# An attention, expert and SwiGLU kernel: four edits to the order of its first 110 microseconds

## The chip, the core and the metric

The kernel runs on one core of one Trainium2 chip. The metric is the device time of one execution in microseconds, the median of the runs made. One more execution was recorded by the hardware profiler; all rows in this document are from it.

## What is computed

Three layers follow each other. First a linear attention with a decaying state, for 2 batches, 8 heads, 768 tokens and a head dimension of 48:

```python
for t in range(S):
    cur = np.einsum('bhd,bhe->bhde', u[None] * kt, vt)
    y[:, :, t] = np.einsum('bhd,bhde->bhe', rt, state + cur)
    state = wt[:, :, :, None] * state + np.einsum('bhd,bhe->bhde', kt, vt)
```

Its output is taken as 1536 tokens of 384 numbers. Each goes to the one of 8 experts with the largest gate logit, in the order of the tokens, as long as the expert has places; an expert is `relu(x @ w1) @ w2` with 1024 hidden numbers, scaled by the token's softmax weight. The last layer is `(silu(x @ w_gate) * (x @ w_val)) @ w_out` with 1536 hidden numbers. Inputs and output are fp32.

## The kernel before, in words

**Stages.** The tokens are cut into 12 units of 128 (u = 0 to 11). The first stage, up to about 108 us, runs the attention, the gate and the placing of tokens; the eight experts follow, then the last layer. The order of the instructions of each engine is the order in which the code issues them; `tc.manual_schedule()` leaves it alone. Tiles come from rotating buffers, and each instruction waits on semaphores for what it reads and overwrites.

**One unit of attention.** VectorE turns the decays into running products: `prep1` (line 363 `X`, a scan; 368 `anch`) and `prep2` (406 `R`, a scan; 412 and 415 `M`; 425 `rk`). TensorE multiplies keys with queries in `scores` (460, `psA`), ScalarE copies them out (462) and GpSimd blanks the upper triangle (463, `A`). `kgtok` turns the keys (471). `values` (485 and 490, `y`) is the attention's output, `state` (502 `psP`; VectorE 505 `d`, 510 `Sa`, 513 `Sc`) carries the state to the next unit, `expand` copies it (521, `Sb`). Each token's own term comes from `diag` and `columns`: a product with `fold` (570) into the small tile `lg`, copied by ScalarE (572, `a`), multiplied with the values by `own` (440, `aV`, on GpSimd). `xrow` (527) adds both into the unit's row `x`. `gate_t` turns it (541), `logits` (565) multiplies by the gate.

**The loop.** The loop over u = 0 to 9 does, in this order: `xrow(u-1)`, `state(u)`, idle products on TensorE (`warm`, line 449: 128 by 512 columns, read by nobody), `scores(u+1)`, `kgtok(u+1)`, `prep1(u+2)`, `gate_t(u-1)`, `prep2(u+2)`, `values(u)`, `columns` and `own` for u+1. Groups of units (0 to 3, 4 to 7, 8 and 9, 10 and 11) are chosen and counted together (`choose`, `count`, `place`), and `scatter` writes their weighted rows `xg` to their experts' places in DRAM (`scr`), by an indirect DMA on GpSimd's queue.

**The tail** (u = 10, written out by hand) finishes units 10 and 11. Expert 0's rows do not go through DRAM for units 8 to 11: `onehot` (790, `hot`) builds a matrix from a unit's places, and `x0_add` (810) sums row times matrix into three PSUM tiles `x0`. The rows of units 0 to 7 are loaded back from `scr` (`x0_load`, 784, into `zrow`) and added by a product with the identity. For units 10 and 11 a row is split into two fp32r halves, `x0_high` (799, ScalarE) and `x0_low` (804, VectorE). Units 8 and 9 use the fp32 row `xg`. `parts` (815, 816) splits the sum into `xe`, which expert 0 multiplies (1270, `psh`).

**Weights.** SyncE's queue loads raw weights (169, 768 KB each) into rotating buffers. ScalarE makes the high half (207), VectorE the low half (212) into `wu`; `fill(us)` places as many such steps as a budget allows. Buffers freed by `early.close()` allow three more raw loads.

Of the kernel before, what the change touches and what calls it, by code (L numbers as in the profile page):

```python
# [33 lines left out]
RAWS = 5, 2, 3  # L34
# [8 lines left out]
def build(tc, cap, dm, tk, vt, ub, cst, wg, w1, w2, wgate, wval, wout, out):  # L43
# [738 lines left out]
    def x0_load():  # L782
        for a, (s0, n) in enumerate(PARTS):
            nc.sync.dma_start(out=zrow[0:n, DM * a:DM * a + DM], in_=scr[s0:s0 + n, :])
# [82 lines left out]
    for u in range(NU - 2):  # L867
# [3 lines left out]
        if u:  # L871
            prep0(u + 2)
        warm((7, 4)[u] if u < 2 else 3, ps1, "xT")
        scores(u + 1)
# [25 lines left out]
        if u:  # L900
            values(u)
            columns(u - 1, max(u - 2, 0), u + 1)
            own(u + 1)
        else:
            values(u, [0, 1])
            for q in range(2):
                columns(q, q, q)
                own(q)
            values(u, [2, 3])
        if chosen:  # L910
# [30 lines left out]
    prep3(u + 1)  # L941
    early.close()
    more_raws(RAWS[2])
    load_raws(len(raws_))
    values(u, [2])
# [16 lines left out]
    columns(u - 1, u - 2, u + 1)  # L962
    xrow(u)
    rows4[2]()
    own(u + 1, nc.vector)
    gate_t(u)
    values(u + 1, [1, 2])
    c2, sums2, rows2, _ = chosen_of(two)
    for f in c2:
        f()  # L970
    rows4[3]()
    for q in (*ready, *four):
        scatter(q)
    x0_load()
    for f in sums2:
        f()
    count(two)
    at2, bases, placed, later = place(two)
    for f in (*bases, *placed):
        f()  # L980
    fill(1.2, 3.0)
    values(u + 1, [3])
    for f in rows2:
        f()
    xrow(u + 1)
    logits(u)
    for i in range(2):
        onehot(i, *(x[:, i, :] for x in at2))
    gate_t(u + 1)
    x0_add(xgs[two[0]], R(hot[0][:, 0, :]), 0, first=True, ks=[0])  # L990
    judge()
    tc.mark_branch_hint_location("rare", engines=[PE, SP])
    logits(u + 1)
    for f in later:
        f()
    for q in two:
        scatter(q)
    flush()
    fill(0.6, 3.0)
    x0_add(xgs[two[0]], R(hot[0][:, 0, :]), 0, first=True, ks=[1, 2])  # L1000
    c, sums, rows, sm = chosen_of(last)
# [4 lines left out]
    for f in (*bases, *sums):  # L1006
        f()
    tc.mark_branch_hint_location("rare", engines=[DVE, ACT, POOL])
    for i, q in enumerate(last):
# [5 lines left out]
    totals(ps1, ones, (ohacc, *(ohs[:, q, :] for q in (*two, *last))), odds)  # L1015
    x0_add(xgs[two[1]], R(hot[0][:, 1, :]), 0)
    for i, q in enumerate(last):
# [3 lines left out]
    x0_add(xhl[last[0]][1], hot[0][:, 2, :], 0)  # L1021
    offsets(one8)
    for f in rows:
        f()
# [499 lines left out]
```

## Time and profile before

| | |
|---|---|
| median of 3 runs | 473.61 us (472.63 to 474.22) |
| the profiled execution | 477.16 us, its span 475.4 us |
| TensorE matmul busy | 454.4 us (96%) |
| VectorE busy | 335.0 us (70%) |
| ScalarE busy | 239.8 us (50%) |
| mean granted TensorE clock | 0.976 of full speed |

A busy time of matmuls says that TensorE had some in flight, not that it ran at its peak, so stages are read one by one: which engine is busy all the time in a stretch, and what ends the waits of the others. In the page's slices of the span the granted clock is below full speed in three places, at about 19 to 26, 70 to 74 and 94 to 105 us. The two levels of TensorE's clock are 1.2 and 2.4 GHz. In the rows, PE is TensorE's matmul, DVE VectorE, ACT ScalarE, POOL GpSimd and SPq SyncE's DMA queue; L490 is line 490 of the kernel before.

### The profile page before, as it was taken

What the parts mean: (1) busy time and instruction counts of PE and PEld (TensorE: products, weight loads), DVE (VectorE), ACT (ScalarE), POOL (GpSimd) and SP (SyncE); (2) the same over time, 40 slices, a digit from 0 to 9 for tenths busy, and PEclk for the clock granted to TensorE, in tenths of its full rate; (3) what the DMA queues carried; (4) which work ended last, traced back from release to release, by engine and by line L of the source; (5) the groups of instructions that cost most, each with busy time, mean ns of one, the idle gap of its engine ahead of it and who ended that gap; (6) DMA issues with size and microseconds to landing.
All of it is one profiled execution on the core that took longest, in us unless ns stands there. A gap on an engine that the chain in (4) does not pass through costs nothing.

```text
span 475.4 us, 9312 instructions
## 1 busy us (share of the span) xinstructions
PE 454.4 (96%) x3572; PEld 401.8 (85%) x3572; DVE 335.0 (70%) x723; ACT 239.8 (50%) x560; POOL 72.6 (15%) x87
## 2 busy tenths in 40 slices
PE   7899889888999999999999999999999999999994
PEld 3587668678999999999988888888888888888884
DVE  8889999677798658559779966575868576434241
ACT  4466676636788677665455465353625333221220
POOL 3334445621000000000000370000000000003033
PEclk9899998959999999999999999999999999999999
DMA  7877996564989965027323425042200000001011
GB/s 241 234 236 205 361 270 186 184 215 135 293 272 345 305 239 175 24 67 219 115 77 123 71 64 122 11 123 77 66 2 1 1 0 0 1 0 68 0 68 66
DMA packets 33649, 62.57 MB, mean 132 GB/s; under 512 B 5216, under 2 KB 16992, under 8 KB 33600
## 3 DMA queue, kind: packets, MB, share of 16 engines
q1 hardware_dynamic: 31680, 57.20, 39.2%
q0 software_dynamic: 1920, 4.73, 2.7%
q8 instruction: 29, 0.48, 0.4%
q14 instruction: 20, 0.16, 0.1%
HBM read 52.48 MB, written 9.44 MB: 130 GB/s over the span
## 4 chain that ended last, share of the span: by engine, by line
PE 79%; DVE 10%; issue 4%; ACT 2%; DMA 2%; POOL 1%; another core or an unknown queue 0%; POOLq 0%; SPq 0%; DVEq 0%; ACTq 0%
PE psg L1381 31%; PE psu L1404 14%; PE psh L1270 14%; PE pso L1288 14%; DVE R L406 2%; DVE X L363 1%; PE psA L460 1%; DMA scr<-zrow 1%; POOL out L1416 1%; DVE M L415 1%; DVE M L412 1%; PE psx L1255 1%; PE y L490 1%; PE psW L449 1%; DVE rk L425 1%
## 5 line engine op out<-in xcount | busy, mean ns | idle before, releaser
L1381 PE MATMUL psg<-yb,wu 128*128 128x512 f32 x648 | 156.3, 395 | 0.0
L1381 PEld LDWEIGHTS psg<-yb,wu 128*128 128x128 f32 x648 | 121.5, 188 | 26.0
L1404 PE MATMUL psu<-wu,a 128*128 128x384 f32 x432 | 80.8, 336 | 0.0
L1404 PEld LDWEIGHTS psu<-wu,a 128*128 128x128 f32 x432 | 76.4, 188 | 2.9
L1270 PE MATMUL psh<-xe,wu 128*128 128x240 f32 x576 | 69.1, 277 | 1.4 <-DVE xe L816 1.4
L1270 PEld LDWEIGHTS psh<-xe,wu 128*128 128x128 f32 x576 | 66.2, 190 | 1.7 <-issue 1.6
L1288 PE MATMUL pso<-h,wu 128*128 128x240 f32 x576 | 66.4, 275 | 0.0
L1288 PEld LDWEIGHTS pso<-h,wu 128*128 128x128 f32 x576 | 65.3, 190 | 0.0
L1388 DVE TENSOR_TENSOR t<-t,psg 128x512 f32<-128x512 f32 x36 | 24.7, 686 | 52.6 <-PE psg L1381 35.6
L212 DVE TENSOR_TENSOR wu<-raw,wu 128x512 fp32r<-128x512 f32 x96 | 61.7, 683 | 0.0
L207 ACT CAST wu<-raw 128x512 fp32r<-128x512 f32 x96 | 55.0, 620 | 3.1 <-PE pso L1288 1.4
L1393 ACT CAST a<-t 128x512 fp32r<-128x512 f32 x36 | 22.3, 618 | 58.2 <-DVE t L1388 55.9
L1277 DVE SCALAR_TENSOR_TENSOR h<-psh,h 128x240 fp32r<-128x240 f32 x64 | 25.0, 403 | 24.1 <-ACT h L1276 23.8
L1303 POOL DMA_INDIRECT idl<-ids,dests x12 | 13.5, 1122 | 163.6 <-DVE bits L187 160.3
L1416 POOL DMA_INDIRECT out<-acc,idc x12 | 11.7, 973 | 174.1 <-DVE acc L1414 172.3
L207 ACT CAST wu<-bits 128x384 fp32r<-128x384 f32 x36 | 18.0, 514 | 40.0 <-DVE bits L200 39.2
L1387 ACT ACTIVATE t<-psg 128x512 f32<-128x512 f32 x36 | 21.4, 596 | 27.5 <-PE psg L1381 27.5
L1394 DVE TENSOR_TENSOR a<-t,a 128x512 fp32r<-128x512 f32 x36 | 24.8, 689 | 11.7 <-ACT a L1393 11.0
L1276 ACT ACTIVATE h<-psh 128x240 fp32r<-128x240 f32 x64 | 23.2, 372 | 11.0 <-PE psh L1270 10.2
L1414 DVE TENSOR_TENSOR acc<-psu,acc 128x384 f32<-128x384 f32 x24 | 12.9, 558 | 20.8 <-PE psu L1404 20.8
L462 ACT COPY A<-psA 128x512 f32<-128x512 f32 x24 | 12.9, 588 | 25.3 <-PE psA L460 23.0
L463 POOL TENSOR_SCALAR_AFFINE_SELECT A<-A 128x512 f32<-128x512 f32 x24 | 19.5, 834 | 27.5 <-ACT A L462 27.5
(153 smaller groups left out, 566.9 us busy)
## 6 DMA issues: line engine op xcount, KB each, us to landing
raw<-in_moe_w SPq DMA_DIRECT2D x32, 768.0 KB, 9.0
dm<-in_dm SPq DMA_DIRECT2D x18, 291.0 KB, 6.1
scr<-zrow SPq DMA_DIRECT2D x12, 384.0 KB, 5.4
raw<-in_moe_w_gate SPq DMA_DIRECT2D x6, 768.0 KB, 5.9
raw<-in_moe_w_val SPq DMA_DIRECT2D x6, 768.0 KB, 4.3
raw<-in_moe_w_out SPq DMA_DIRECT2D x6, 768.0 KB, 4.3
v<-in_tk SPq DMA_DIRECT2D x12, 192.0 KB, 6.7
dm<-in_dm SPq DMA_DIRECT2D x3, 512.0 KB, 5.7
```

Source lines behind the costliest of these rows:

```text
L207: nc.scalar.copy(out=slot_t[u % NSLOT][:, 0, c:c + n], in_=bits[i])
L212: nc.vector.tensor_tensor(out=w[:, 1, c:c + n], in0=bits.pop(i), in1=R(w[:, 0, c:c + n]), op=ALU.subtract)
L1270: nc.tensor.matmul(ps, w[:, a, k, c0:c0 + 128], xet[e][:, b, k, :], start=n == 0, stop=n == 8)
L1276: nc.scalar.activation(out=h[:, 0, :], in_=ps, func=AF.Relu)
L1277: nc.vector.scalar_tensor_tensor(out=h[:, 1, :], in0=ps, scalar=0.0, in1=R(h[:, 0, :]), op0=ALU.max, op1=ALU.subtract)
L1288: nc.tensor.matmul(ypt[e, d], w[:, a, f % 4, 128 * d:128 * d + 128], h[:, b, :], start=f == 0 and n == 0, stop=f == 7 and n == 2)
L1381: nc.tensor.matmul(gps[i][g], w[:, a, g, k, c0:c0 + 128], yb[t, k][:, c], start=a_ == k == 0, stop=a_ == k == 2)
L1387: nc.scalar.activation(out=t, in_=pg[0], func=AF.Silu)
L1388: nc.vector.tensor_tensor(out=t, in0=t, in1=pg[1], op=ALU.mult)
L1393: nc.scalar.copy(out=a[:, 0], in_=t)
L1394: nc.vector.tensor_tensor(out=a[:, 1], in0=t, in1=R(a[:, 0]), op=ALU.subtract)
L1404: nc.tensor.matmul(out_ps[t, j], att[i][:, c, 128 * j:128 * j + 128], w[:, a, f % 4, :], start=f % FP == 0 and n == 0, stop=f % FP == FP - ...
```

## The change

Four edits, in the words of the code.

1. In the loop's first turn `values(0)` is issued whole, ahead of both products with `fold`, in place of half ahead and half behind. The two products write 8 columns each instead of 16, with no copy between them; one copy takes both results.
2. From u = 2 on, `warm` issues five idle products instead of three; two more stand in the tail.
3. `early.close()` and the three raw loads stand behind `x0_load` instead of ahead of it.
4. Units 8 and 9 enter `x0` as fp32r halves, as 10 and 11 do, and their `xg` rows, places (`later`) and scatters come later. Two steps of `fill` move: one ahead, in front of `own(u+1)`, one behind `offsets`.

```diff
--- before.py
+++ after.py
@@ -870,7 +870,7 @@
         state(u)
         if u:
             prep0(u + 2)
-        warm((7, 4)[u] if u < 2 else 3, ps1, "xT")
+        warm((7, 4)[u] if u < 2 else 5, ps1, "xT")
         scores(u + 1)
         expand(u)
         kgtok(u + 1)
@@ -902,11 +902,15 @@
             columns(u - 1, max(u - 2, 0), u + 1)
             own(u + 1)
         else:
-            values(u, [0, 1])
+            values(u)
             for q in range(2):
-                columns(q, q, q)
+                to = logits_to(q)
+                nc.tensor.matmul(to[:, 0:E], gss.pop(q), fold[:, E:2 * E], start=True, stop=True)
+            a8 = gp.tile([128, 2, H], F32, tag="a82", name="a82")
+            nc.scalar.copy(out=a8, in_=lgt[group[0]][:, 0:2, 0:E])
+            for q in range(2):
+                a8s[q] = a8[:, q, :]
                 own(q)
-            values(u, [2, 3])
         if chosen:
             flush()
             if u < NU - 3:
@@ -939,9 +943,6 @@
     count(four)
     xrow(u - 1)
     prep3(u + 1)
-    early.close()
-    more_raws(RAWS[2])
-    load_raws(len(raws_))
     values(u, [2])
     gate_t(u - 1)
     place(four)
@@ -961,43 +962,47 @@
     logits(u - 1)
     columns(u - 1, u - 2, u + 1)
     xrow(u)
+    fill(1.2, 3.0)
     rows4[2]()
     own(u + 1, nc.vector)
     gate_t(u)
     values(u + 1, [1, 2])
-    c2, sums2, rows2, _ = chosen_of(two)
+    c2, sums2, rows2, sm2 = chosen_of(two)
     for f in c2:
         f()
     rows4[3]()
     for q in (*ready, *four):
         scatter(q)
     x0_load()
+    early.close()
+    more_raws(RAWS[2])
+    load_raws(len(raws_))
     for f in sums2:
         f()
     count(two)
     at2, bases, placed, later = place(two)
     for f in (*bases, *placed):
         f()
-    fill(1.2, 3.0)
     values(u + 1, [3])
-    for f in rows2:
-        f()
+    for i, q in enumerate(two):
+        x0_high(q, sm2[:, i, :])
     xrow(u + 1)
     logits(u)
+    warm(2)
     for i in range(2):
         onehot(i, *(x[:, i, :] for x in at2))
     gate_t(u + 1)
-    x0_add(xgs[two[0]], R(hot[0][:, 0, :]), 0, first=True, ks=[0])
+    x0_add(xhl[two[0]][0], hot[0][:, 0, :], 0, first=True)
+    for i, q in enumerate(two):
+        x0_low(q, sm2[:, i, :])
+    for f in rows2:
+        f()
     judge()
     tc.mark_branch_hint_location("rare", engines=[PE, SP])
     logits(u + 1)
-    for f in later:
-        f()
-    for q in two:
-        scatter(q)
-    flush()
-    fill(0.6, 3.0)
-    x0_add(xgs[two[0]], R(hot[0][:, 0, :]), 0, first=True, ks=[1, 2])
+    x0_add(xhl[two[1]][0], hot[0][:, 1, :], 0)
+    for i, q in enumerate(two):
+        x0_add(xhl[q][1], hot[0][:, i, :], 0)
     c, sums, rows, sm = chosen_of(last)
     for f in c:
         f()
@@ -1005,6 +1010,11 @@
     atl, bases, placed, after = place(last)
     for f in (*bases, *sums):
         f()
+    flush()
+    for f in later:
+        f()
+    for q in two:
+        scatter(q)
     tc.mark_branch_hint_location("rare", engines=[DVE, ACT, POOL])
     for i, q in enumerate(last):
         x0_high(q, sm[:, i, :])
@@ -1013,13 +1023,13 @@
     for i in range(2):
         onehot(2 + i, *(x[:, i, :] for x in atl))
     totals(ps1, ones, (ohacc, *(ohs[:, q, :] for q in (*two, *last))), odds)
-    x0_add(xgs[two[1]], R(hot[0][:, 1, :]), 0)
     for i, q in enumerate(last):
         x0_add(xhl[q][0], hot[0][:, 2 + i, :], 0)
     for i, q in enumerate(last):
         x0_low(q, sm[:, i, :])
     x0_add(xhl[last[0]][1], hot[0][:, 2, :], 0)
     offsets(one8)
+    fill(0.6, 3.0)
     for f in rows:
         f()
     for f in after:
```

How this stands on the engines, in three places. First TensorE in the loop's first turn: `y` is the attention's output of unit 0, `lg` the products with `fold`, `gs` what they read, `psP` the state's product.

```order
 L449 MATMUL psW<-xinit,ones 128x512
-L490 MATMUL y<-v,A 64x48 x8
-L570 MATMUL lg<-fold,gs 128x16 x2
-L490 MATMUL y<-v,A 64x48 x8
+L490 MATMUL y<-v,A 64x48 x16
+L908 MATMUL lg<-fold,gs 128x8 x2
 L502 MATMUL psP<-v,kgt 64x48 x8
```

The two products with `fold` moved from between the two halves of the 16 value products to behind them (in a trace each fp32 product has two records).

Second, ScalarE in the tail, behind the copy `a` that VectorE's own term of unit 11 waits for: `wu` are the high halves of weights, `xg` weighted rows, `xT` the turned row, `ex` the exponentials of units 8 and 9.

```order
 L585 ACTIVATE xg<-x,sm 128x384
-L572 COPY a_1564<-lg 128x8
+L572 COPY a_1568<-lg 128x8
+L207 CAST wu_82<-raw 128x512 x2
 L585 ACTIVATE xg<-x,sm 128x384
 L546 COPY xT<-psx 128x384
 L611 ACTIVATE ex<-ls 128x16
```

Two casts of weights, which stood behind the next `xg`, now stand ahead of the turned row and of the exponentials.

Third, VectorE in the tail, where units 10 and 11 are placed: `sm` is the softmax sum, `t`, `sl` and `hot` lead to the matrix of places.

```order
 L580 RECIPROCAL sm<-sm 128x2
-L695 TENSOR_TENSOR t_1716<-lg,ohs 128x16
-L670 TENSOR_REDUCE sl<-t_1716 128x2
+L383 TENSOR_SCALAR within<-within 128x1
+L386 TENSOR_SCALAR odds<-within 128x1
+L680 COPY pcs<-lg 128x16
+L700 TENSOR_SCALAR end_1649<-sl 128x2
+L703 TENSOR_TENSOR end<-end,sl 128x2
+L706 TENSOR_TENSOR slots<-end,end_1649 128x2
+L695 TENSOR_TENSOR t_1732<-lg,ohs 128x16
+L670 TENSOR_REDUCE sl<-t_1732 128x2
 L790 TENSOR_SCALAR hot<-col,end,sl 128x240 x2
```

Six short steps (the finiteness test, and the places of units 8 and 9) moved in between the reciprocal and the first step towards the places of units 10 and 11.

## Rows read from the trace of the kernel before

**Rows 1.** Busy time by stretch: the stretch, its length, then the engines and the clock.

```profile
17.00:27.00 10.00, 7.77 (x74) 5.46 (x69) 8.10 (x19) 4.26 (x18) 1.85 (x3) 0.66 0.96 311
94.00:105.00 11.00, 7.85 (x40) 6.60 (x41) 8.26 (x37) 3.82 (x10) 2.18 (x3) 0.53 0.70 247
44.00:86.00 42.00, 38.10 (x638) 29.63 (x634) 41.48 (x96) 27.46 (x83) 20.91 (x24) 0.96 0.84 250
109.00:473.00 364.00, 360.38 (x2274) 330.99 (x2274) 239.84 (x478) 177.99 (x377) 25.14 (x24) 1.00 0.33 102
```

**Rows 2.** Timeline, 15 to 32 us: start, length, engine, line, operation; waits in brackets.

```profile
16.45 0.67 PE L490 MATMUL y<-v,A 128*64 128x48 f32 x16
18.35 0.40 PE L570 MATMUL lg<-fold,gs 128*128 128x16 f32 x2 [1.24 <-ACT gs L886]
19.74 0.60 PE L570 MATMUL lg<-fold,gs 128*128 128x16 f32 x2 [0.99 <-ACT a L572]
19.77 1.68 POOL L440 TENSOR_TENSOR aV<-v,a 128x384 f32<-128x384 f32 x2 [3.04 <-ACT a L572]
20.27 1.10 PE L490 MATMUL y<-v,A 128*64 128x48 f32 x16
21.49 0.56 DVE L527 TENSOR_TENSOR x<-y,aV 128x384 f32<-128x384 f32 x1 [1.72 <-POOL aV L440]
22.94 1.30 DVE L363 TENSOR_TENSOR_SCAN X<-dm,xinit 128x264 f32<-128x264 f32 x2
23.97 2.08 PE L460 MATMUL psA<-M 64*128 64x128 f32 x16
29.35 0.56 DVE L527 TENSOR_TENSOR x<-y,aV 128x384 f32<-128x384 f32 x1 [1.27 <-PE y L490]
30.21 0.36 DVE L510 TENSOR_TENSOR Sa<-psP,Sc 128x192 f32<-128x192 f32 x1 [0.23 <-PE psP L502]
```

**Rows 3.** Chain of work that ended last, 24 to 40 us: start, length, piece.

```profile
36.30 0.75 PE psW L449 x3
```

**Rows 4.** Timeline, 24 to 37 us, VectorE and GpSimd.

```profile
25.78 0.67 DVE L412 TENSOR_TENSOR M<-dm,X 128x512 f32<-128x512 f32 x1
32.70 1.93 POOL L463 TENSOR_SCALAR_AFFINE_SELECT A<-A 128x512 f32<-128x512 f32 x2 [1.97 <-ACT A L462]
34.11 1.05 DVE L412 TENSOR_TENSOR M<-dm,X 128x512 f32<-128x512 f32 x1
```

**Rows 5.** Timeline, 89 to 112 us, the last units and expert 0's first products.

```profile
90.54 0.56 DVE L440 TENSOR_TENSOR aV<-v,a 128x384 f32<-128x384 f32 x1 [1.01 <-ACT a L572]
91.50 0.21 ACT L611 ACTIVATE ex<-ls 128x16 f32<-128x16 f32 x1
92.13 1.12 ACT L207 CAST wu<-raw 128x512 fp32r<-128x512 f32 x2
95.04 0.17 DVE L695 TENSOR_TENSOR t<-lg,ohs 128x16 f32<-128x16 f32 x1 [2.28 <-remote]
95.34 1.28 DVE L212 TENSOR_TENSOR wu<-raw,wu 128x512 fp32r<-128x512 f32 x2
96.54 0.55 DVE L527 TENSOR_TENSOR x<-y,aV 128x384 f32<-128x384 f32 x1
100.16 0.17 DVE L606 TENSOR_REDUCE mx<-lg 128x2 f32<-128x16 f32 x1 [0.36 <-PE lg L565]
102.18 0.17 DVE L695 TENSOR_TENSOR t<-lg,ohs 128x16 f32<-128x16 f32 x1
106.80 0.41 DVE L816 TENSOR_TENSOR xe<-x,xe 128x240 fp32r<-128x240 f32 x1 [1.23 <-issue]
108.89 3.29 PE L1270 MATMUL psh<-xe,wu 128*128 128x240 f32 x27 [1.40 <-DVE xe L816]
```

**Rows 6.** Timeline, 89 to 112 us, GpSimd's last early scatter and SyncE's loads.

```profile
93.53 0.97 POOL L735 DMA_INDIRECT scr<-xg,slots  x1 [0.30 <-ACT wu L207]
98.18 2.08 SPq L784 DMA_DIRECT2D zrow<-scr  x2
```

## The prediction

> **What bounds the kernel now.** I read four views. First the busy time by stretch [rows 1]: from 109 to 473 us TensorE's matmul is busy 360.38 of 364.00 us at a granted clock of 1.00. None of the four edits takes work out of that stretch, so the change is worth what it moves expert 0's first product, which starts at 108.89 us [rows 5]. From 44 to 86 us VectorE is busy 41.48 of 42.00 us and TensorE 38.10: there VectorE sets the pace, and TensorE has some 3.9 us to spare. In 17 to 27 us and 94 to 105 us the clock stands at 0.66 and 0.53 of full speed: most of these stretches ran at 1.2 GHz, the lower level. Second the timeline of the first turns [rows 2], third the chain of waits [rows 3], where TensorE's idle products are links, fourth the timeline of the tail [rows 5, 6], to see which wait ends last ahead of 108.89 us.
>
> **How the profiled execution stands to the runs.** It took 477.16 us, the median run 473.61: 3.55 more. In it VectorE's step at 95.04 us waited 2.28 us for something that the profile does not name [rows 5]; the products it reads had no wait in the code that could last so long. After it TensorE ran at the lower clock [rows 1]. I take that the timed runs mostly lack this stall, so a gain that comes from its absence counts in the profiled execution and not in the median.
>
> **Edit 1, the first turn.** Before: half of the values at 16.45 us (0.67 us), then TensorE waits 1.24 us for `gs` and 0.99 us for the copy `a` between the two products, and the other half runs at the lower clock from 20.27 us (1.10 us against 0.67) [rows 2]. The lower clock came after these two gaps. Now 2 x 0.67 us of values run from 16.45 to 17.8 us, the wait for `gs` shrinks to some 0.5 us, the one for `a` goes. Both products end at about 18.9 us, `psP` follows (0.67 us before the change at full clock, as the values), four idle products at 0.25 each (three in 0.75 us, [rows 3]), and `psA` starts at 18.9 + 0.7 + 1.0 = 20.6 us instead of 23.97: TensorE is 3.4 us ahead. VectorE gains less. Its row `x` waited until 21.49 us for the values' end (20.27 + 1.10) and for GpSimd, whose two `aV` take 1.68 us from 19.77. The values are now long done, the first `aV` ends at 19.77 + 0.84 = 20.6 us: 0.8 us earlier (none, if `x` must wait for both). The scan `X` of 22.94 us moves with it. The next `x` waited 1.27 us for TensorE's values and the next `Sa` 0.23 us for `psP`; with TensorE 3.4 us ahead both waits go. VectorE is then 0.8 + 1.5 = 2.3 us ahead at about 31 us. From there it is packed, so I carry 2.3 us to the tail. Bounds: 1.5 without the first term; 3.2 if the whole 1.72 us wait at 21.49 goes with the 1.5; nothing, if something else in the packed stretch (a late transfer, GpSimd) takes it back.
>
> A trace of that last case is in the rows: `M` takes 0.67 us at 25.78 and 1.05 us at 34.11, where GpSimd's blanking runs from 32.70 for 1.93 us [rows 4]. The Trainium skill, "SBUF — State Buffer", section "SBUF: two separate sides", says that VectorE operations with two SBUF inputs and GpSimd operations that read SBUF take one shared port pair in turn, each for its whole length. The trace agrees in sign, though an operation that met a 1.93 us pair lost 0.38 us only. By that rule moving TensorE against VectorE moves the blanking onto other VectorE steps, and the sum would be 0.4 us less or more for each turn whose meeting changes; by the row alone, where each turn has one meeting before and after, nothing.
>
> **Edit 2, idle products.** Two more in each of eight turns, at 0.75 / 3 = 0.25 us [rows 3], are 8 x 0.5 = 4.0 us of TensorE. Three of these turns lie before 44 us: 1.5 us, covered by the 3.4 us that edit 1 puts TensorE ahead. Five lie in 44 to 86 us: 2.5 us, inside the 3.9 us to spare there [rows 1]. I take nothing. The other end is 4.0 us, if neither cover holds. Should they keep the clock higher there (0.96), this also gives nothing, since VectorE sets the pace; the two in the tail stand where TensorE waits for `x`.
>
> **Edit 3, raw loads.** Before, the last early scatter was issued at 93.53 us and SyncE's loads of `zrow` started at 98.18, 4.65 us later, with the three raw loads under way [rows 6]. Now the scatter is alone and the raws follow. `zrow` is read only at the end of the sum, so a faster scatter gives nothing; the raws that arrive later belong to expert 1, whose products come only behind all of expert 0's. I take nothing, and keep 0 to 2 us of loss for scatters and loads of the tail that now meet the raws. The Trainium skill, "DMA: Bandwidth & Descriptors", section "Queues, rings and completion order", says that a DMA engine takes packets in turn from the queue rows that have work. By that rule the raws now share with the scatters of units 8 to 11 instead of 4 to 7, and these need at most the 4.65 us of the row; expert 1's rows are turned later than that.
>
> **Edit 4 and the moved steps, the tail.** I follow VectorE, without the 2.3 us. (a) Two `wu` steps (1.28 us) leave the place ahead of `x` at 96.54 us and go in front of `aV` at 90.54, into a wait of 1.01 us: +0.3 there, -1.28 here. (b) On ScalarE the two casts (1.12 us) now stand ahead of `ex`: 91.50 becomes 92.6, the sum behind it waits, +1.1 us. (c) The 2.28 us stall goes. `x` comes at 96.54 - 1.28 + 1.1 - 2.28 = 94.1 us (the 0.3 lies inside the 1.1) [rows 5]. (d) From `x` to `mx` passed 100.16 - 96.54 = 3.6 us, with TensorE at the lower clock [rows 1]; I take 2 us of it as products, which at full clock are 1 us less: `mx` at 94.1 + 2.6 = 96.7. The new fp32r halves lie beside it: both `x0_high` on ScalarE before the row is turned, both `x0_low` on VectorE while it waits for the logits. (e) From `mx` to `t` were eleven short steps in 102.18 - 100.16 = 2.0 us, 0.18 each; six more are at most 1.1, I take 0.8, as not all depend on each other: `t` at 96.7 + 2.8 = 99.5 instead of 102.18. (f) From `t` to `xe` passed 4.6 us, with 1.23 us in which VectorE waited for TensorE, behind in its sums at the lower clock. Without it 3.4, plus the third `wu` step (0.64) that now stands there: `xe` at 103.5. (g) From `xe` to the first product passed 2.1 us, now some 1.8, as the three `xe` steps no longer wait for TensorE: 105.3 instead of 108.89, a gain of 3.6 us, 2.28 of it the stall.
>
> **The sum.** Against the profiled execution: 2.3 + 0 + 0 + 3.6 = 5.9 us, 471.3 us. For the median the stall is left out: 473.61 - (5.9 - 2.28) = 470.0. If all of the 3.55 us by which the profiled execution is longer belonged to the stall and the lower clock behind it, only 5.9 - 3.55 = 2.35 us would be left: 471.3. I take a point between, nearer to the second since the lower clock came with the stall: 471.0 us.
>
> **Rivals.** (A) The stall belongs to the kernel, comes in every run, and goes with the raw loads that were under way there ahead of `zrow` [rows 6]: then all 5.9 us count, 467.7. For it: the raws' traffic is the one thing special there. Against: the runs are 3.55 us faster than the profiled execution. (B) The gain is given back in the tail. If the timed runs had the full clock there, (d), (f) and (g) give nothing and the six steps (0.8) and the `wu` step (0.64) cost 1.4, against 1.28 - 1.1 gained: +1.2 us; with 1.5 of the front left, 473.3, no change. For it: (b) and (e) put work on VectorE's chain. (C) Slower: the idle products make TensorE the bound. The place is the turns from u = 2; the price is 4.0 us less whatever waits TensorE still has; it decides once the front's lead on TensorE is under 1.5 us, as it would be if the clock falls again at 19 us. With half of the products uncovered (+2.0), the tail's +1.2 and no gain in front: 476.8. Against: TensorE's 3.9 us to spare. (D) The first edit does not do what it says: `x` waits for both `aV` and the clock falls all the same. Some 1 us of the two waits would still go; 472.6.
>
> **How the numbers follow.** The forecast (470.0 to 472.0, my own range 469.0 to 472.2) gets 0.50, A 0.17, B 0.15, D 0.08, C 0.10. The 8 in 10 range goes from A's 467.6 to past B's, 473.8; it leaves out most of C and a little below A. A measurement of this kernel can tell 0.3%, 1.42 us: faster is below 472.19. Forecast and A nearly whole give 0.65; B, D and a rest of the forecast 0.24 for the same; C and some of B 0.11 for slower.
>
> **What would show it.** Right: no stretch at 1.2 GHz near 20 us; the second `psA` at about 20.6 us, the scan `X` at about 22 and the `Sa` of 30.21 us some 2.3 us earlier, at about 27.9; VectorE still packed from 44 to 86 us; no wait of TensorE's for the places at 94 to 105 us longer than 1 us, clock 1.00 there; the first expert product at 103 us. Wrong: VectorE waiting for TensorE (`psP`, `y`) in the middle turns would show C; a first product at 105 us or later at full clock shows B; a wait of TensorE's on raw weights behind 109 us would break edit 3's nothing.

## The result and the profile after

The changed kernel takes 480.37 us in the median, against 473.75 for the kernel before: ratio 1.0125, 95% interval 1.0079 to 1.0172. (Its four runs are 477.83, 479.81, 480.93 and 743.04; in the last TensorE's mean clock was 0.557, and the ratio leaves it out: the median of the other three is 479.81.) Forecast were 471.0 us and a range of 467.6 to 473.8: the sign was wrong and the time lies outside. The profiled execution took 479.81 us, with a span of 478.0.

Up to expert 0's first product nearly all steps came when they were forecast. Busy time by stretch, after (stretch, length, PE, PEld, DVE, ACT, POOL, clock, DMA share, GB/s), answering to [rows 1]; the fourth line is a stretch not shown before:

```profile
17.00:27.00 10.00, 8.72 (x138) 6.43 (x136) 9.09 (x19) 7.22 (x27) 4.56 (x5) 1.00 0.99 244
44.00:86.00 42.00, 37.20 (x621) 28.46 (x621) 41.48 (x100) 26.82 (x82) 21.20 (x25) 1.00 0.88 242
94.00:105.00 11.00, 8.05 (x64) 7.64 (x64) 7.54 (x37) 4.87 (x13) 3.90 (x4) 0.84 0.79 255
105.00:120.00 15.00, 10.96 (x67) 10.07 (x66) 5.90 (x13) 5.34 (x13) 0.00 (x0) 0.77 0.53 182
109.00:473.00 364.00, 359.72 (x2238) 329.55 (x2238) 239.59 (x478) 177.77 (x377) 24.19 (x23) 0.99 0.32 100
```

The clock is 1.00 from 17 to 27 us (0.66 before) and VectorE is packed from 44 to 86, both as forecast. From 94 to 105 us the clock is 0.84, where 1.00 was forecast. And from 105 to 120 us, where before TensorE was busy 13.61 of 15 us at full clock, it is now busy 10.96 us at 0.77. The front, answering to [rows 2], timeline (start, length, engine, line, operation, wait):

```profile
20.23 1.16 PE L460 MATMUL psA<-M 64*128 64x128 f32 x16
...
20.41 0.56 DVE L527 TENSOR_TENSOR x<-y,aV 128x384 f32<-128x384 f32 x1 [0.87 <-POOL aV L440]
...
21.76 1.69 DVE L363 TENSOR_TENSOR_SCAN X<-dm,xinit 128x264 f32<-128x264 f32 x2
...
22.14 1.75 POOL L463 TENSOR_SCALAR_AFFINE_SELECT A<-A 128x512 f32<-128x512 f32 x2 [0.98 <-ACT A L462]
...
27.96 0.35 DVE L510 TENSOR_TENSOR Sa<-psP,Sc 128x192 f32<-128x192 f32 x1
```

The second `psA` was forecast for 20.6 us, `X` for about 22, `Sa` for 27.9. The tail, answering to [rows 5]:

```profile
94.63 0.18 DVE L606 TENSOR_REDUCE mx<-lg 128x2 f32<-128x16 f32 x1 [0.20 <-PE lg L565]
...
101.43 0.41 DVE L816 TENSOR_TENSOR xe<-x,xe 128x240 fp32r<-128x240 f32 x1 [0.43 <-ACT xe L815]
...
103.85 4.30 PE L1280 MATMUL psh<-xe,wu 128*128 128x240 f32 x36 [1.25 <-ACTq L1219]
110.48 0.37 ACT L1286 ACTIVATE h<-psh 128x240 fp32r<-128x240 f32 x1 [7.48 <-SPq L1219]
...
111.35 1.01 PE L1280 MATMUL psh<-xe,wu 128*128 128x240 f32 x4 [3.19 <-DVE h L1287]
```

With the front's 2.3 us taken off, the forecast steps were `mx` 94.4, `xe` 101.2, first product 103.0 us; the rows say 94.63, 101.43, 103.85. Then comes what no step had: ScalarE's first `h` waits 7.48 us, and not for its product. TensorE runs 36 products (nine for each of the four places in PSUM that hold `psh`, 4.30 us), finds no place free, and stands 3.19 us. Behind this wait the clock falls: from 112.2 to 119.0 us it is at 1.2 GHz. What is waited for is SyncE's queue at line 1219, the rare branch (taken only when an expert gets more tokens than its 240 places; the join is where both ways meet behind it). SyncE's queue from 94 to 99 us, timeline:

```profile
95.56 2.32 SPq L169 DMA_DIRECT2D raw<-in_moe_w  x4
```

The last of these four, from the view of the transfers issued between 97.05 and 97.2 us (KB, us from issue to landing):

```profile
raw<-in_moe_w SPq DMA_DIRECT2D x1, 768.0 KB, 13.2
```

The fourth is issued at 97.09 us and lands 13.2 us later, at 110.27; `h` starts at 110.48. In the program's order the first instruction of ScalarE and the first of VectorE behind the branch wait for all eight semaphores of SyncE's loads:

```
443 L1219 UNCONDITIONAL_BRANCH [waits Activation_49,Activation_sequencer_49]
444 L1286 ACTIVATE h_5763<-psh_5743 128x240 [waits DMAHW3_49,DMAHW4_49,DMAHW2_49,DMAHW5_49,DMAHW1_49,DMAHW6_49,DMAHW0_49,DMAHW7_49,PE_49,Activation_49]
```

The wait stands in the kernel before too, but there the last raw load, issued at 100.30 us, landed at 104.53, ahead of the first product at 108.89.

These rows account for the loss. From the first product to the end of the span pass 374.15 us (478.0 - 103.85), against 366.56 in a second profile of the kernel before (b_again below, 469.9 - 103.34): 7.6 us more. TensorE's wait for `h` is 3.2 us of it, two waits for VectorE's `wu` steps behind it 0.9 us, and a clock of 0.77 over 15 us is worth 3.45 us (an estimate: 15 x 0.23).

### The profile page after: what moved, and what is told of

Same layout as the page of the kernel before. It is cut to its first block, busy times and chain, and to the rows that moved or that the text cites. A ratio compares the mean times of both kernels' runs of the same rounds, so it can differ in the third digit from the quotient of the medians.

```text
span 478.0 us, 9339 instructions
## 1 busy us (share of the span) xinstructions
PE 453.3 (95%) x3579; PEld 400.6 (84%) x3590; DVE 336.6 (70%) x725; ACT 240.6 (50%) x561; POOL 73.0 (15%) x87
## 4 chain that ended last, share of the span: by engine, by line
PE 72%; issue 2%; DVE 1%; POOL 1%; POOLq 0%; ACT 0%; ACTq 0%
PE psg L1391 31%; PE psu L1414 14%; PE pso L1298 14%; PE psh L1280 13%; POOL out L1426 1%; PE psx L1265 1%; DVE acc L1424 0%; DVE wu L212 0%; POOLq L1530 0%; DVE h L1287 0%; ACT h L1286 0%; POOLq L1426 0%; ACTq L1286 0%
## 5 line engine op out<-in xcount | busy, mean ns | idle before, releaser
L1280 PE MATMUL psh<-xe,wu 128*128 128x240 f32 x576 | 72.6, 284 | 5.3 <-DVE h L1287 3.2
L1280 PEld LDWEIGHTS psh<-xe,wu 128*128 128x128 f32 x576 | 68.9, 196 | 6.4 <-DVE h L1287 3.4
```

The lines of the kernel that those rows point to most:

```text
L1280: nc.tensor.matmul(ps, w[:, a, k, c0:c0 + 128], xet[e][:, b, k, :], start=n == 0, stop=n == 8)
```

## The experiments

Theory J: the raw loads, moved to the end of SyncE's list, are what the join behind the branch waits for. Rivals: L, a late semaphore (an event that tells of finished work and comes late); T, the raws' traffic wherever it stands. For the gains that did not show: F, the first profile of before was not typical; K, edit 4 opens empty stretches for TensorE, and the lower clock that follows falls on the tail. N, the rival of K: the clock costs nothing there. P: the edits do what the prediction says. Runs of one group share a chip with runs of the kernel before; there were three chips. Medians in us; "first" is the start of expert 0's first product, "low" the stretches between 86 and 120 us at 1.2 GHz, all in the profiled execution, which can lie some us off its median. The row f_after is the changed kernel, unedited.

| run | edits | median | before beside it | ratio, 95% interval | first | first `h` | low |
|---|---|---|---|---|---|---|---|
| b_again | none | 471.63 (one run) | 472.81 | | 103.34 | 104.70 | 95.3–98.7 |
| a_no3 | 1, 2, 4 | 475.11 | 472.81 | 1.0043, 1.0023–1.0062 | 106.47 | 108.03 | 91–104.6 |
| b_only3 | 3 | 480.75 | 472.81 | 1.0168, 1.0144–1.0193 | 103.48 | 111.13 | 95.6–99, 112.6–119.5 |
| a_behind | 1, 2, 4, raws behind the join | 473.15 | 472.81 | 1.0006, 0.9988–1.0024 | 104.77 | 107.13 | 97.6–107.9 |
| b_only1 | 1 | 472.82 | 473.34 | 0.9988, 0.9976–1.0001 | 104.44 | 105.80 | 93.6–100.4 |
| b_only2 | 2 | 474.69 | 473.34 | 1.0032, 1.0013–1.0050 | 105.76 | 107.12 | 94.9–101.7 |
| b_only4 | 4 | 475.61 | 473.34 | 1.0048, 1.0030–1.0066 | 106.57 | 108.94 | 101.3–111.5 |
| b_behind | raws behind the join | 473.69 | 473.34 | 1.0002, 0.9987–1.0016 | 104.38 | 105.94 | 93.1–99.9 |
| v1_warm4 | 1, four idle products | 472.48 | 472.94 | 0.9988, 0.9977–0.9998 | 104.02 | 105.58 | none |
| v4_early_fill | as v1, `wu` steps early | 472.60 | 472.94 | 0.9996, 0.9980–1.0011 | 104.99 | 107.35 | 102.1–108.9 |
| a_behind_warm | as a_behind, six idle products | 472.07 | 472.94 | 0.9980, 0.9966–0.9994 | 102.58 | 103.93 | none |
| d4 | all four, six idle products | 477.77 | 477.15 | 1.0028, 1.0011–1.0045 | 104.51 | 110.60 | 96–99.4, 113.1–119.9 |
| d3 | d4, one raw behind | 474.51 | 477.15 | 0.9962, 0.9947–0.9977 | 106.05 | 107.41 | 95.2–102.1 |
| d2 | d4, two raws behind | 474.03 | 477.15 | 0.9951, 0.9933–0.9968 | 107.53 | 109.03 | 93.9–104.1 |
| d_old | 1, 2, 4, six idle products | 476.11 | 477.15 | 0.9992, 0.9971–1.0013 | 107.32 | 109.68 | 93.6–100.5, 107.3–110.7 |
| f_d2 | d2 again | 471.67 | 473.47 | 0.9966, 0.9953–0.9980 | 102.55 | 105.49 | none |
| f_old | d_old again | 472.28 | 473.47 | 0.9980, 0.9965–0.9995 | 103.67 | 105.22 | none |
| f_after | the change | 480.01 | 473.47 | 1.0147, 1.0120–1.0174 | 104.84 | 111.21 | 97.1–103.9, 114.2–117.6 |

**b_again.** Nothing is edited.

> The kernel before once more, unchanged, for a second profile of it. If the 2.28 us that VectorE waited at 95.04 us in the first profile belong to that one execution, they are missing here, the first product of expert 0 starts at 105 to 106 us instead of 108.89, and the profiled execution takes 473 to 475 us. If they belong to the kernel, the wait is there again and the product starts at about 109 us.

Busy time of two stretches of it, with the clock third from the end:

```profile
17.00:27.00 10.00, 7.93 (x104) 5.67 (x105) 8.59 (x19) 5.58 (x21) 3.33 (x4) 0.83 0.99 233
94.00:105.00 11.00, 9.71 (x71) 8.55 (x71) 7.09 (x36) 4.92 (x14) 3.55 (x4) 0.84 0.70 242
```

Its front, timeline:

```profile
22.18 1.30 DVE L363 TENSOR_TENSOR_SCAN X<-dm,xinit 128x264 f32<-128x264 f32 x2
...
28.66 0.36 DVE L510 TENSOR_TENSOR Sa<-psP,Sc 128x192 f32<-128x192 f32 x1 [0.23 <-PE psP L502]
```

And its first product with the first `h`:

```profile
103.34 1.83 PE L1270 MATMUL psh<-xe,wu 128*128 128x240 f32 x14 [1.16 <-ACTq L1209]
...
104.70 0.37 ACT L1276 ACTIVATE h<-psh 128x240 fp32r<-128x240 f32 x1 [2.12 <-PE psh L1270]
```

Theory F holds, and by more than it said (105 to 106 us, 473 to 475 us): the wait of 2.28 us is missing, the clock is 0.83 and 0.84 in the two stretches (0.66 and 0.53 in [rows 1]), the second `Sa` comes 1.55 us earlier than in [rows 2], and the first product 5.55 us earlier than in [rows 5]. The profiled time falls with it, 477.16 to 471.63. Against this profile the changed kernel gains nothing at its first product: 103.85 against 103.34 us. But b_again is no typical execution either: it lies at the lower end of the 23 runs beside it (471.57 to 474.44, median 472.81). So a difference of about 1 us against its rows needs the medians beside it.

**a_no3, b_only3, a_behind.** `load_raws` (and its pool) is put back; put behind `x0_load` in the kernel before; and put behind the join:

```diff
     x0_load()
     early.close()
-    more_raws(RAWS[2])
-    load_raws(len(raws_))
...
     x_load(1)
+    more_raws(RAWS[2])
+    load_raws(len(raws_))
```

> The changed kernel with the raw loads back at their old place (edit 3 undone). Theory J (the join behind the rare branch: the first instruction of ScalarE and of VectorE behind it waits until every load that SyncE has issued has landed, the last raw weights with them): the last raw load lands before 105 us, the first h of ScalarE follows its product (at about 105.5 us, no wait for SyncE), TensorE has no idle stretch of 3 us behind 104 us, 470.5 to 473 us. Theory L (a semaphore of TensorE came late by chance of the program, as the 2.28 us before): the wait of some 7 us is there again, 478 to 481 us. Theory T (the raw traffic slows whatever runs beside it): traffic now lies at 87 to 97 us and slows the scatters there, zrow comes 3 us later, 474 to 477 us.

> The kernel before with edit 3 alone. Theory J: the four raw loads are issued behind zrow from about 97 us, the last lands at 110 to 113 us, the first h starts 0.2 us behind that landing, TensorE idles 2 to 4 us once its four places are full and falls to the lower clock; 477 to 481 us. Theory L: edit 3 does nothing by itself, 473 to 474.5 us. Theory T: slower too, but the first h is not tied to the landing of the last raw load.

> The changed kernel with the pool of the last three raw buffers opened, and its loads issued, behind the join and the load of expert 1's rows; one raw load (into a buffer that came free) stays ahead of the join. Theory J: the load ahead of the join lands by about 104 us, no wait for SyncE at the first h, the scatters land in 2.5 to 3 us instead of 6.3 to 7.6, first product at 103.5 to 104.5, 470.5 to 472.5 us. Theory T: the same bytes now flow while expert 0 is worked on, so the wait moves and stays: 476 to 480 us. Theory L: the wait of 7 us is there again, 478 to 481 us.

The first `h` and the next product after TensorE's stand in b_only3, timeline:

```profile
111.13 0.37 ACT L1276 ACTIVATE h<-psh 128x240 fp32r<-128x240 f32 x1 [8.52 <-SPq L1209]
...
111.99 1.15 PE L1270 MATMUL psh<-xe,wu 128*128 128x240 f32 x4 [4.22 <-DVE h L1277]
```

Edit 3 alone costs 7.9 us (480.75 - 472.81), and its last raw load lands at 110.91 us, 0.22 ahead of this `h`. With the loads at their old place or behind the join no `h` waits for SyncE. L and T fall: one because edit 3 alone makes the wait, the other because behind the join the same bytes cost nothing. But a_no3, without the wait, is still slower than before, against J's own number, and a_behind (473.15) misses J's 470.5 to 472.5 too. T's number is met (474 to 477), not its mechanism: `zrow` has landed at 101.11 us, and its first product starts at 102.64. What is low is the clock (stretch from 94 to 105 us):

```profile
94.00:105.00 11.00, 10.14 (x60) 9.71 (x59) 7.00 (x36) 5.14 (x13) 2.50 (x3) 0.52 0.62 220
```

Edits 1, 2 and 4 together lose 2.3 us. They don't add to edit 3's 7.9: with all four the kernel takes 480.01 us (f_after) and with edit 3 alone 480.75, as in both the end hangs on the last landing.

**b_only1, b_only2, b_only4, b_behind.** The kernel before with one edit each, by that edit's lines of the change's diff: the first turn; `else 5` for `else 3` in the turns' `warm`; all of the tail but the raws' move; and the move shown last, behind the join.

> The kernel before with edit 1 alone. Theory F (the first profile of before showed a bad front: in the second one the scan X of unit 2 starts at 22.18 us, and edit 1 has little left to gain): no stretch at 1.2 GHz at 20 to 24 us, second psA 2.5 to 3 us earlier than 23.22, but X of units 6 and later within 0.5 us of the second profile of before, 472 to 473.2 us against 472.8. Theory P (the prediction): VectorE stays 2.3 us ahead through the packed stretch, x of the last unit at 90 to 91 us, 470.3 to 471 us.

> The kernel before with five idle products instead of three in the turns from u = 2 (the two in the tail are not among them). If they are covered: X and x of the middle turns as in the second profile of before within 0.3 us, 472.3 to 473.3 us. Theory C (they make TensorE the bound, as its lead is small there): VectorE waits for psP and y in these turns, x of the last unit 1 to 2.5 us later, 474 to 476 us.

> The kernel before with edit 4 and the moved steps of the tail alone, the two idle products of the tail with them; the raw loads stay at their old place, the first turn and the three idle products as before. Theory K (the new order leaves TensorE without work ahead of the last rows' products, and the lower clock falls on these, on zrow's and on expert 0's first): a stretch at 1.2 GHz between 91 and 107 us that is longer than the 3 us of the second profile of before, first product at 104.5 to 107 us, 473.5 to 476 us. Theory P (the prediction): the tail is 1.3 us shorter, first product by 102.3 us, 471 to 472 us.

> The kernel before with the last raw buffers opened, and their loads issued, behind the join and the load of expert 1's rows. Theory J: no wait for SyncE at the first h; scatters of units 4 to 7 land in 2.6 us instead of 4.7 to 6.8, zrow by 97.5 us, which nothing waits for; first product at 103.3 us as in the second profile of before; 471.8 to 473.2 us, no difference. If the raw traffic had slowed the tail of before, 470 to 471.5 us.

Edit 1 gives 0.5 us, and its interval takes in no change. (The scan `X` of 22.18 us in b_again, which the text above gives to unit 2, is unit 3's.) In b_only1 the `Sa` of 28.66 us (b_again) comes at 28.06, and the `X` of unit 11, the last, at 77.57 against 77.75: a lead of 0.6 us shrinks to 0.2 while VectorE is packed. Edit 2 alone costs 1.35 us, though VectorE waits no longer than before for `psP` and `y` (only 1.48 against 1.22 us at the first `x`); its steps themselves get longer (from 20 to 58 us `d` 1.8 us against 1.1, `X` 8.3 against 7.9, `R` 8.1 against 7.9), and `X` of unit 7 comes at 49.70 against 48.68. Why they do was not tested. On top of edit 1 it costs nothing by the rows: `X` of unit 11 stands at 77.48 in the changed kernel and at 77.57 in b_only1. Edit 4 alone costs 2.3 us. The products of the last rows and expert 0's first in b_only4, timeline of TensorE:

```profile
99.78 1.97 PE L810 MATMUL x<-hot,xhl 128*128 128x240 f32 x10 [0.87 <-DVE hot L790]
...
106.57 1.64 PE L1276 MATMUL psh<-xe,wu 128*128 128x240 f32 x6 [1.15 <-ACTq L1215]
```

TensorE stands 0.85 us from 97.77 us and 0.87 from 98.91, both ahead of the last rows; from 101.3 to 111.5 us the clock is at 1.2 GHz. In b_again TensorE has no such empty places there: the fp32 products of units 8 and 9 (1.95 us from 95.27, 2.05 from 97.46), which edit 4 turns into cheaper halves and moves ahead, fill them. Its lower clock came behind a wait of 1.13 us for `x`, and was over by 98.7. From the last `x` to the first product pass 12.87 us here, 10.55 there; but the execution profiled here is 1.55 us over its median, and b_again 1.2 under its own, so the 2.3 us of the medians are the price. b_behind shows that the raws' traffic at their old place did not slow the tail of before.

**v1_warm4, v4_early_fill, a_behind_warm.** Idle products in the empty places: four behind `logits(u)` on edit 1 alone; the same with `fill(1.2, 3.0)` early; three on each side of `totals` on a_behind:

```diff
     logits(u)
+    warm(4)
...
+    warm(3, ps1, "T")
     totals(ps1, ones, (ohacc, *(ohs[:, q, :] for q in (*two, *last))), odds)
+    warm(3, ps1, "T")
```

> Edit 1 alone, with four idle products (1.0 us at full clock) put where TensorE waits 1.13 us for x of the last unit. Theory K (an empty stretch of about 1 us in the tail is followed by the lower clock, and the lower clock on the tail's products is what the tail's length hangs on): no stretch at 1.2 GHz between 92 and 103 us, first product 0.7 to 1.5 us earlier than the 104.44 of edit 1 alone, 471 to 472 us against 472.8 there. Rival N (the lower clock costs nothing there, since VectorE sets the tail): no change against edit 1 alone, 472.5 to 473.2 us.

> The kernel of the run before this one, with the two wu steps of the tail moved in front of the last aV, as in the change. If the prediction's step (a) holds by itself, x of the last unit comes 0.5 to 1.0 us earlier than 92.6 and the first product with it: 470.5 to 471.7 us, 0.5 us or more under the run before this one. If the wait only moves to the next step (TensorE's products or the choice's steps), the same within 0.4 us.

> The changed kernel with its raw loads behind the join, and three idle products in each of the two places of 0.84 and 0.87 us in which TensorE has nothing ahead of the last rows' products. Theory K: the lower clock of 97 to 107 us goes, zrow's products take 0.6 us instead of 1.04 each, first product at 103 us or earlier instead of 104.77, 471 to 472 us against 473.15 without them. Rival N (the lengths of edit 4 are VectorE's and ScalarE's, not the clock's): 472.7 to 473.6 us.

TensorE in v1_warm4, timeline:

```profile
100.82 0.93 PE L810 MATMUL x<-ident,zrow 128*128 128x128 f32 x4 [0.52 <-DMA zrow<-scr]
...
104.02 1.26 PE L1275 MATMUL psh<-xe,wu 128*128 128x240 f32 x7 [1.15 <-ACTq L1214]
```

Busy time from 94 to 105 us in a_behind, without idle products:

```profile
94.00:105.00 11.00, 8.14 (x55) 7.65 (x56) 7.61 (x38) 4.99 (x13) 4.58 (x4) 0.66 0.55 180
```

And in a_behind_warm, with them:

```profile
94.00:105.00 11.00, 9.48 (x81) 7.80 (x81) 8.05 (x39) 5.80 (x16) 3.88 (x4) 1.00 0.52 180
```

TensorE's only long wait behind 103 us there (us in total, times, longest):

```profile
PE psx L1265 <- DMA xr<-scr: 0.9, 1, 0.9
```

K holds in a_behind_warm: full clock, first product 2.19 us earlier than in a_behind, 1.1 us in the median (a_behind's profiled execution is 1.4 us over its median). A new wait of 0.9 us stands behind it, where TensorE waits for expert 2's rows, whose load stands behind the late raws. In v1 the tail's clock is full too, yet K's number is missed: the ratio to the kernel before is 0.9988, as for b_only1. TensorE now waits for `zrow`, which lands at 101.23 us with the raws at their old place (99.57 in b_only1, 98.23 in b_behind). In v4 that wait is 1.15 us, and the lower clock comes behind it, in an execution 2.5 us over its median: a miss, the earlier `x` (92.36 against 92.93) buys nothing.

**d4, d3, d2, d_old.** The number of raw loads ahead of the join, with a cap in `load_raws`, on the tail with six idle products:

```diff
-        while st["loaded"] < min(upto, len(raws_)):
+        while st["loaded"] < min(upto, len(raws_), st["cap"]):
```

> The changed kernel with its four raw loads where the change puts them, and six idle products in the two empty places of the tail. Theory J: first product at 102.6 us, last raw load landed at about 110, first h 0.2 us behind it; TensorE idles some 3.5 to 4 us, then falls to the lower clock: 478.5 to 480.5 us, as without the idle products (480.4), since the end is set by the landing.

> As the run before this one, but three raw loads ahead of the join and the fourth behind the load of expert 1's rows. Theory J: the third lands at 106 to 108.5 us, first h 0.2 us behind, TensorE idles 0 to 2 us: 473 to 477 us, between the neighbours. Theory T (the price is the traffic and not the join): as with four, 478 to 480 us.

> As before, but two raw loads ahead of the join and two behind. Theory J: the second lands at 103.5 to 104.5 us, within 0.6 us of the time at which the first h could start anyway (103.9): no idle time of TensorE, 471 to 472 us, 0 to 1 us under the run with one load ahead (472.07), since the loads of expert 2's rows stand in a shorter queue.

> The changed kernel with the raw loads at their old place and the six idle products. Without the idle products it took 475.1 us, with 13 us at the lower clock. Theory K: the lower clock goes, first product at 103 to 104 us (zrow lands at about 101 us, some 1 us late), 471.5 to 472.7 us. Rival N: 474.5 to 475.5 us.

These four runs were on a chip of their own, on which the kernel before takes 477.15 us, as in its first profile (477.16). On the other chips its runs took 471.55 to 474.44. All four profiles have a wait at the place of that profile's 2.28 us; in d_old:

```profile
93.64 0.17 DVE L695 TENSOR_TENSOR t<-lg,ohs 128x16 f32<-128x16 f32 x1 [1.76 <-PE psW L449]
```

So this wait goes with the chip, as far as five profiles tell, and not with raw loads: in d4, d3 and d2 none is issued between 78 and 95 us. First `h` in d4, timeline:

```profile
110.60 0.37 ACT L1288 ACTIVATE h<-psh 128x240 fp32r<-128x240 f32 x1 [6.86 <-SPq L1221]
```

And in d3:

```profile
107.41 0.37 ACT L1289 ACTIVATE h<-psh 128x240 fp32r<-128x240 f32 x1 [2.11 <-PE psh L1283]
```

With four loads ahead `h` follows the last landing (110.39) by 0.21 us; with three it lands at 106.72 and `h` waits 2.11 us for its product only. J's step is a maximum of two times, not a sum, and with the first product 2 to 5 us later here than in f_d2 below three loads were already free. d2's 474.03 us, on this chip, miss the forecast. d_old says nothing on K, and misses its number: the wait empties TensorE by itself (1.88 us from 92.66).

**f_d2, f_old, f_after.** d2, d_old and the changed kernel, unedited, on a chip without that wait.

> The kernel with two raw loads ahead of the join, two behind, and six idle products in the tail, once more. Theory J with K: where the before beside it is near 473 us, no wait ahead of the last unit's x, first product at 102.6 us, first h not held by a load, 471 to 472 us. Where the before is near 477, again 0.5% under it.

> The changed kernel with the raw loads at their old place and the six idle products, once more. Theory K: with a before near 473 us, no stretch at 1.2 GHz in the tail, zrow lands at about 101 us and holds TensorE some 1 us, first product near 103.5 us, 472 to 473.5 us. Rival N: 474.5 to 475.5 us.

> The changed kernel itself, beside the other two. Theory J: the last raw load lands at 110 to 111 us and the first h follows it by 0.2 us whatever the tail did: 477.5 to 481 us in either case, so 1.0 to 1.5% over a before near 473 and 0 to 0.8% over one near 477.

First product, first `h` and TensorE's next stand in f_d2, timeline:

```profile
102.55 4.78 PE L1283 MATMUL psh<-xe,wu 128*128 128x240 f32 x40 [1.15 <-ACTq L1222]
...
105.49 0.37 ACT L1289 ACTIVATE h<-psh 128x240 fp32r<-128x240 f32 x1 [3.69 <-SPq L1222]
...
107.87 0.38 PE L1283 MATMUL psh<-xe,wu 128*128 128x240 f32 x1 [0.54 <-DVE wu L212]
```

Busy time from 94 to 105 us in f_old, where a_no3 had the clock at 0.52:

```profile
94.00:105.00 11.00, 8.88 (x70) 6.72 (x70) 7.43 (x37) 4.86 (x13) 2.73 (x3) 1.00 0.62 214
```

That idle products pay is shown: with them, edits 1, 2 and 4 go from 2.3 us slower than before (a_no3) to 1.2 us faster (f_old), with intervals far apart. The timed runs' own mean granted clocks go with it: their median is 0.9865 in a_no3 and 0.9975 in f_old, 0.993 in a_behind and 0.996 in a_behind_warm. That the two empty places alone bring the lower clock is not shown. In a_behind, after, f_after and b_only4 it came at the first of them or behind; in a_no3 it came at 91.0 us, ahead of both. There TensorE had stood 0.61 us, but in f_old it stood 0.62 us at the same step and the clock held. TensorE in a_no3, then in f_old, timeline:

```profile
90.77 0.18 PE L643 MATMUL lg<-ohs,tri 128*128 128x8 bf16 x1 [0.61 <-DVE ohs L620]
...
90.52 0.18 PE L643 MATMUL lg<-ohs,tri 128*128 128x8 bf16 x1 [0.62 <-DVE ohs L620]
```

J is shown too: f_after's last raw load lands at 111.00, `h` at 111.21, as in after. f_d2 beats both kernels, 471.67 us: 1.8 under before, 8.3 under the change. Its second raw load still holds `h`, against the expectation: `h` starts 0.38 us behind the landing at 105.11, and TensorE then waits twice for VectorE's `wu` steps, 1.1 us in all.

## Why the prediction was wrong, step by step

**What bounds the kernel.** Right that the stretch behind expert 0's first product is fixed, wrong that therefore "the change is worth what it moves expert 0's first product": that product came 5.04 us earlier in the profiles and the end 2.6 us later. The first product of TensorE doesn't wait for the join's loads; the first `h` of ScalarE does, and after 36 products the one stops the other.

**Edit 3** is the step that failed: "I take nothing, and keep 0 to 2 us of loss". It asked who reads the raws (expert 1, late: true) and what shares the queues, not who waits for SyncE's queue as a whole. Measured alone: 7.9 us. The prediction's sign for this, a wait of TensorE's "on raw weights behind 109 us", came in another form: TensorE's wait, at 108.16 us, was for `h`. The place to see it is the wait list of the first `h`, in the program's order; in the trace of before it ended before the product did and so left no row. In the Trainium skill, "DMA: Bandwidth & Descriptors", section "Queues, rings and completion order", packets of several queue rows are taken in turn; the trace agrees that loads share: the four scatters issued from 98 to 104 us, beside the raws, took 6.9 us in the median, by the view of the transfers:

```profile
scr<-xg,slots POOLq DMA_INDIRECT x4, 6.9
```

In b_again, with one raw load left beside them, those issued from 100 to 106 us took 3.2 us by the same view. The prediction's cap of 4.65 us for them was too low. The last landed at 109.52 us, ahead of the last raw load.

**How the profiled execution stands to the runs.** The prediction left out 2.28 of the 3.55 us, and weighed all of it as a lower bound. The wait was indeed not the kernel's: it is missing in b_again, where the first product starts 5.55 us earlier and the time is 5.53 us less. As b_again is 1.2 us under its median, and the lower clock differs between the two as well, the 3.55 us can't be split further; that the lower bound was the better choice is argued. Rival A, which tied the wait to the raw loads, falls with d4 to d2; D falls with the front's rows.

**Edit 1.** Each row came as worked out, within 0.4 us, but the 2.3 us were counted against a front with its clock at 0.66. Against b_again it is 0.7 us at the second `Sa` and 0.3 us from unit 7 on. Of the rest, part is taken back, as the lower bound had it ("if something else in the packed stretch", GpSimd among them, "takes it back"). VectorE's long steps of the changed kernel from 20 to 44 us by line (after the bar: busy us, mean ns of one):

```profile
L363 DVE TENSOR_TENSOR_SCAN X<-dm,xinit 128x264 f32<-128x264 f32 x8 | 6.8, 886 | 0.0
L415 DVE TENSOR_TENSOR M<-dm,R 128x512 f32<-128x512 f32 x3 | 4.0, 1318 | 0.0
L406 DVE TENSOR_TENSOR_SCAN R<-wm,anch 128x256 f32<-128x256 f32 x6 | 3.7, 664 | 0.0
...
L425 DVE TENSOR_TENSOR rk<-dm 128x512 f32<-128x512 f32 x3 | 2.0, 679 | 0.0
L412 DVE TENSOR_TENSOR M<-dm,X 128x512 f32<-128x512 f32 x3 | 2.0, 667 | 0.0
```

And of b_again:

```profile
L363 DVE TENSOR_TENSOR_SCAN X<-dm,xinit 128x264 f32<-128x264 f32 x8 | 5.2, 690 | 0.0
L406 DVE TENSOR_TENSOR_SCAN R<-wm,anch 128x256 f32<-128x256 f32 x6 | 4.6, 806 | 0.0
L415 DVE TENSOR_TENSOR M<-dm,R 128x512 f32<-128x512 f32 x3 | 2.5, 828 | 0.0
L425 DVE TENSOR_TENSOR rk<-dm 128x512 f32<-128x512 f32 x3 | 2.5, 824 | 0.0
L412 DVE TENSOR_TENSOR M<-dm,X 128x512 f32<-128x512 f32 x3 | 2.4, 792 | 0.0
```

`X` and the `M` of line 415 take 3.1 us more, `R` 0.9 less (with `rk` and the other `M`, another 0.9 less). b_only1 has the changed kernel's figures for all five, so they are edit 1's. GpSimd's steps now meet other VectorE steps: `X` of 21.76 us stands beside the blanking of 22.14. The Trainium skill, "SBUF — State Buffer", section "SBUF: two separate sides", has the two engines take one port pair in turn. The prediction's sentence on it, 0.4 us for each turn whose meeting changes, was the better account: 1.3 us more over three turns by these rows. The row that it weighed against the rule was read short: the blanking of 32.70 ends at 34.63, so the `M` of 34.11 met only 0.52 us of it, and the two `R` of 32.55 lost as much (1.64 us, where those of 30.69 in the changed kernel take 1.24). That it is this port is argued from rows; no run took GpSimd's steps away.

**Edit 2.** "I take nothing" holds on top of edit 1 and only there; alone it costs 1.35 us. Rival C had the right sign and the wrong way: VectorE did not wait for TensorE.

**Edit 4.** The times of `x`, `mx`, `t` and `xe` came out within 0.25 us, in part by luck: (e) took 2.47 us instead of 2.8 and (f) 4.33 instead of 4.0, and the two cancel. (g) failed: from `xe` to the first product 2.42 us instead of 1.8, as the first two groups of `zrow`'s products ran at 1.2 GHz (1.04 and 1.02 us each, 0.60 in b_again). Against b_again the tail from the last `x` got longer, 11.87 us against 10.55. The prediction granted the full clock there and asked only about waits longer than 1 us; in the changed kernel the clock fell at 98.49 us, behind waits of 0.84 and 0.86. This is the second step that failed: the tail counted as a gain of 1.3 us against the runs, and edit 4 alone costs 2.3. Rival B had a loss of 1.2 us, for another reason: the runs have the full clock, and the steps on VectorE's chain cost. Its premise fails: in b_again too the tail has 3.4 us at 1.2 GHz.

## What to carry to other kernels

Before a load is moved down a queue, look for the next place that waits for the whole queue, a join, a barrier, a branch, and set the load's landing against the time at which that place is reached; a wait that ends early leaves no row, so it is read from the program and not from the trace. Work made cheaper on TensorE where it waits can lengthen what follows, if the clock then falls; look at the new empty places, and try idle products in them. Where the profiled execution lies outside the timed runs, take a second profile, and set that one against the runs too.

## What was not expected of the hardware

On one chip VectorE's `t` waits 1.0 to 2.3 us for the counts' products in all of four profiles (and in the first one of before, whose time fits that chip), in the other fifteen not at all. In d_old TensorE's products end at 90.91, 91.44 and 92.66 us by their rows (whose ends are modelled), but their semaphore events stand at 93.61, 93.74 and 93.83; the later products start meanwhile, at 91.06 and 92.06. What holds the events back stays open. The lower clock, once there, lasted from 3.4 us (b_again) to 13.6 (a_no3) in much the same tail, and the spread of the timed runs goes with it: over twelve runs 0.6 to 2.5 us in the four kernels whose profile shows none in the tail, 2.5 to 4.9 in the nine whose profile shows some.
